# Sparse attention and a gated feed-forward layer: shared value buffers, dense rows in stage order, another load order, and gathers by indirect transfer

## The chip, the core and the metric

The kernel runs on one core of one Trainium2 chip. The core has five engines that run at the same time, each with its own queue of instructions that it takes strictly in order: TensorE (PE, matrix products and transposes), VectorE (DVE), ScalarE (ACT), GpSimd (POOL) and SyncE (SP), which computes nothing and only issues transfers. Semaphores tie the queues together. The metric is the device time of one execution in microseconds; lower is better.

## The reference

Four batches of eight heads, 768 positions of 64 numbers each. The positions fall into 24 blocks of 32. A query block sees its own block and both neighbours, the first and the last block, and three blocks drawn at random; the first and the last query block see everything:

```python
mask = np.abs(blk_i - blk_j) <= 1
mask = mask | (blk_i == 0) | (blk_j == 0) | (blk_i == 23) | (blk_j == 23)
for qb in range(24):
    for kb in sampled_blocks[qb]:
        mask[qb*32:(qb+1)*32, kb*32:(kb+1)*32] = True
scores = np.where(mask, scale * q @ k.T, -1e9)
attn_out = softmax(scores) @ v
x = attn_out, heads side by side: (3072, 512)
out = (sigmoid(x @ w_gate) * (x @ w_val)) @ w_out        # 512 -> 1536 -> 512
```

All inputs are float32; the kernel computes in 16 bits and accumulates in float32.

## The kernel before, in words

**A planner writes the order.** The kernel builds a list of operations (`P(name, engine, duration, function, deps, prio, ...)`) and simulates them (`Planner.run`, lines 69 to 178). Each has an engine or a choice of two, an assumed duration, dependencies that must have ended (`deps`), dependencies that must only have been issued (`after`), a priority, and buffers that it takes and gives back (`acq`, `rel`). The program is then emitted in the order of the simulation. On the chip each engine follows that list, and waits where the data are not there or a buffer is not free. An `after` is a matter of the list alone, and makes no wait on the chip.

**Attention, one batch after another** (`attention`, lines 430 to 785). `load` (line 348) brings K, Q and V of a batch from float32 in DRAM to 16 bits in one of three stage buffers `stg` (96 partitions; partition p holds rows 8p to 8p+7), issued on POOL. PE transposes K and Q (line 456), DVE or ACT copy the results to `KT` and `QT` (lines 466 to 474). V is rearranged by DVE (`vsh`, line 486), in batch 0 into the space of `XL`, later into another stage buffer, and SP writes it to a scratch area `scr` in DRAM, 768 KB in four transfers (`f_scr`, line 495). From there SP loads three things:

- `VN`, all values of the batch, for the dense rows (line 500);
- windows: for three or four query blocks at once the three neighbouring value blocks, into `V1` (line 542). Each batch has two windows at a time, called A and B; even and odd batches have their own pair (`r = b % 2`);
- gathers: for each query block its three random value blocks, into `V2`, by three transfers whose addresses come from registers (line 587).

The first and the last value block go to one window by DMA (lines 514, 515) and are copied by POOL to the other places (line 522).

For each of the 22 sparse query blocks `i` of a batch, POOL copies the three random key blocks to `KG` (line 573; the first and last block stand there already, lines 530, 531). PE adds a mask row by four small matmuls (line 608) and the scores by eight (line 614), DVE takes the maximum (line 626), ACT the exponential (line 635), DVE the reciprocal, DVE or POOL the scaling (lines 643 to 655), PE transposes (line 666), DVE or ACT copy to `PTS` (line 673), PE multiplies with `V1` and `V2` (line 686), ACT or DVE put the result into `XT` (line 701). Mostly two blocks go as one step. Six `P` buffers and two `PTS` buffers bound how many blocks may be under way.

The dense rows (first and last query block, per pair of heads `p`) have scores against all 768 keys (line 714), softmax, six transposes of 128 columns (line 751), a copy to `DPT` (line 756) and six products with `VN` (line 764). In batch 0 they come at its end, in the others at its start.

**Feed-forward**, in eight groups of 128 to 512 rows: products with `wg` and `wv` (line 814), tanh and combination (lines 822, 827), the product with `wo` (line 840), scaling, and the store, which SP issues (line 854). A group can start when its rows of `XT` are there; the planner puts the groups between attention steps, and the last two mostly behind. The weights come on POOL's queue, in four pairs of chunks and three chunks of `wo` (lines 371, 379). `GATES` (line 295) puts some of them behind the gathers of blocks 7, 9, 10 and 11 of batch 0 in the list.

Where the change and the steps touch the code:

Of the kernel before, what the change touches and what calls it, by code (L numbers as in the profile page):

```python
# [18 lines left out]
BLK = 32  # L19
# [5 lines left out]
TP = 96  # L25
# [156 lines left out]
def kernel(  # L182
# [28 lines left out]
    cst = np.zeros((1, NB, 8), np.float32)  # L211
# [3 lines left out]
    cst_h = nc.inline_tensor(cst, name="bb_cst")  # L215

# [14 lines left out]
    ones = sb("ones", [128, 128], bf16)  # L231
    cst_t = sb("cst", [1, NB, 8], f32)
    sbi = sb("sbi", [1, NB * 3 * 2], i32)
    kidx = sb("kidx", [1, 128], i32)
    vidx = sb("vidx", [1, 128], i32)
# [12 lines left out]
    VN = sb("VN", [128, 6, DM])  # L248
    V1 = {(r, x): sb(f"V1{r}{x}", [128, n, DM]) for r in range(2) for x, n in (("A", 4), ("B", 3))}
    V2 = {(r, x): sb(f"V2{r}{x}", [128, n, DM]) for r in range(2) for x, n in (("A", 4), ("B", 3))}  # L250
# [9 lines left out]
    DPT = [sb(f"DPT{s}", [128, S]) for s in range(2)]  # L260
# [17 lines left out]
    XT = [sb(f"XT{g}", [128, NP, 128 * len(G)]) for g, G in enumerate(GROUPS[:-2])]  # L278
    XT += [XL[:, 0:NP, :], XL[:, NP : 2 * NP, :]]
    V0 = XL.rearrange("p a n -> p (a n)")[0:TP, 0 : H * TJ * D]  # L280
# [6 lines left out]
    W0 = [(4, 4, "A"), (8, 3, "B"), (11, 4, "A"), (15, 3, "B"), (18, 2, "A"), (1, 3, "B"), (20, 3, "A")]  # L287
    W1 = [(1, 3, "B"), (20, 3, "A"), (4, 3, "B"), (7, 4, "A"), (11, 3, "B"), (14, 4, "A"), (18, 2, "B")]
# [7 lines left out]
    WCH, WOH = 4, 3  # L296
    SCALE_ENG, SCALE_DUR = ("POOL", "DVE"), (0.9, 0.42)
# [5 lines left out]
    def f_const_dma(o):  # L303
        pin(nc.sync.dma_start(sbi, sampled_blocks.bitcast(i32).rearrange("(x a) b -> x (a b)", x=1)))
        pin(nc.sync.dma_start(cst_t, cst_h.ap()))
        pin(nc.sync.dma_start(ident, ident_h.ap()))

    c_dma = P("cdma", "SP", 1.9, f_const_dma, prio=-100, lat=2.2)
# [5 lines left out]
    def f_mask(o):  # L314
# [17 lines left out]
        pin(V.tensor_scalar(mrow[0:1, :, 2:5], in0=m3, scalar1=NEG, scalar2=None, op0=ALU.mult))  # L332
        pin(V.tensor_scalar(mrow[0:1, :, 0:2], in0=cst_t[:, :, 3:5], scalar1=NEG, scalar2=None, op0=ALU.mult))
# [74 lines left out]
    FF = {"w": None, "vn": None}  # L408
# [21 lines left out]
    def attention(b, prio0, ldeps):  # L430
# [5 lines left out]
        if b == 0:  # L436
            ldk, hk = load("k", k, b, pp - 0.050, ldeps, np_)
            ldq, hq = load("q", q, b, pp - 0.049, ldk[-1:], np_)
            ldv, hv = load("v", v, b, pp - 0.048, ldq[-1:])
            FF["w"] = weights(ldv[-1])  # L440
        else:
            ldv, hv = load("v", v, b, pp - 0.050, ldeps)
            ldk, hk = load("k", k, b, pp - 0.049, ldv)
            ldq, hq = load("q", q, b, pp - 0.048, ldk)
# [39 lines left out]
        def f_vsh(o):  # L484
            t = by_head(stg[pl.handles[hv][1]])
            pin(nc.vector.tensor_copy(by_row(V0 if b == 0 else stg[o.slots[f"vsh{b}"][1]]), t.rearrange("p h j d -> p j h d")))

        vs = P(f"vsh{b}", "DVE", 1.14, f_vsh, deps=ldv, prio=pp - 0.045, rel=[hv],
               acq=[(f"vsh{b}", [("v0", 0)] if b == 0 else stages)])

        def f_scr(o):
            src = V0 if b == 0 else stg[o.slots[f"vsh{b}"][1]]
            dst = scr[b].rearrange("(b j c) n -> c b j n", j=TJ, c=4)
            for c in range(4):
                pin(nc.sync.dma_start(dst[c], src.rearrange("(b c) (j n) -> c b j n", c=4, j=TJ)[c]))

        sc = P(f"scr{b}", "SP", 2.0, f_scr, deps=[vs], prio=pp - 0.045, dma=2.2, ndma=3, rel=[f"vsh{b}"])

        def f_vn(o):
            pin(nc.sync.dma_start(VN, scr[b].rearrange("(t p) n -> p t n", p=128)))  # L500

        vn = P(f"vn{b}", "SP", 0.5, f_vn, deps=[sc], after=[FF["vn"]], prio=bp - 1.2 + (0.5 if b == 0 else 0), dma=2.3,
               acq=[(f"vn{b}", [("vn", 0)])])
        FF["vn"] = vn

        steps = S0 if b == 0 else S1
        wins = W0 if b == 0 else W1
        step_of = {i: y for y, st in enumerate(steps) for i in st}
        wprio = {}
        for i0, n, x in wins:  # L510
            wprio.setdefault(x, bp + 0.1 * step_of[i0] - 1.5)
        vfl = {}
        def f_fl(o):
            pin(nc.sync.dma_start(V1[r, "A"][96:128, 0, :], scr[b][0:BLK, :]))
            pin(nc.sync.dma_start(V2[r, "A"][0:BLK, 0, :], scr[b][S - BLK : S, :]))

        fl = P(f"vfl{b}", "SP", 1.0, f_fl, deps=[sc] + v_users[b - 2], prio=min(wprio.values()) - 0.05, dma=0.2, ndma=2)
        for x, n in (("A", 4), ("B", 3)):
            def f_fc(o, x=x, n=n):
                n0 = 1 if x == "A" else 0  # L520
                for vt, ps in ((V1, slice(96, 128)), (V2, slice(0, BLK))):
                    pin(nc.gpsimd.tensor_copy(
                        vt[r, x][ps, n0:n, :].bitcast(f32),
                        vt[r, "A"][ps, 0:1, :].bitcast(f32).broadcast_to([BLK, n - n0, DM // 2])))

            vfl[x] = P(f"vfc{b}{x}", "POOL", 2.0, f_fc, deps=[fl], prio=wprio[x] - 0.05)

        def f_kfl(o):
            for s in range(NKG):
# [370 lines left out]
```

## Time and profile before

| | us |
|---|---|
| median of the runs (367.83 to 373.71) | 369.97 |
| the profiled execution | 371.52 |
| its span, first to last instruction | 369.6 |
| TensorE busy | 326.2 |
| VectorE busy | 256.0 |
| ScalarE busy | 218.3 |
| GpSimd busy | 106.8 |
| mean granted TensorE clock | 0.957 |

A page of the profile gives busy time by engine, forty slices of the span (each digit the busy tenths of a slice of 9.24 us), the chain of work that ended last, and groups of instructions by source line with what ended the idle time before them. Further views are cut from the same trace: busy time by stage, one engine's instructions in order of time, waits, and transfers. An engine name with a q (SPq, POOLq) stands for instructions that only issue or count and are not busy time.

### The profile page before, as it was taken

What the parts mean: (1) busy time and instruction counts of PE and PEld (TensorE: products, weight loads), DVE (VectorE), ACT (ScalarE), POOL (GpSimd) and SP (SyncE); (2) the same over time, 40 slices, a digit from 0 to 9 for tenths busy, and PEclk for the clock granted to TensorE, in tenths of its full rate; (3) what the DMA queues carried; (4) which work ended last, traced back from release to release, by engine and by line L of the source; (5) the groups of instructions that cost most, each with busy time, mean ns of one, the idle gap of its engine ahead of it and who ended that gap; (6) DMA issues with size and microseconds to landing.
All of it is one profiled execution on the core that took longest, in us unless ns stands there. A gap on an engine that the chain in (4) does not pass through costs nothing.

```text
span 369.6 us, 11338 instructions
## 1 busy us (share of the span) xinstructions
PE 326.2 (88%) x3904; PEld 203.1 (55%) x3904; DVE 256.0 (69%) x686; ACT 218.3 (59%) x662; POOL 106.8 (29%) x361
## 2 busy tenths in 40 slices
PE   2745968989789689999799999999999999999995
PEld 2634756757666544566366556555655654444442
DVE  8697747778688869689469999668989833402320
ACT  3566546774687746767477777877775653313321
POOL 8457470116333553212005234002574100000000
PEclk9995789999999869999899999999999999999999
DMA  7947899997979893125343623331133430011002
GB/s 123 205 115 208 156 212 231 218 243 157 228 188 203 165 268 73 45 67 162 101 118 109 168 73 98 115 94 38 46 89 87 139 104 2 1 59 57 0 30 86
DMA packets 47262, 45.09 MB, mean 122 GB/s; under 512 B 5986, under 2 KB 44132, under 8 KB 47204
## 3 DMA queue, kind: packets, MB, share of 16 engines
q1 hardware_dynamic: 31956, 30.20, 28.8%
q0 software_dynamic: 15248, 14.16, 24.4%
q8 instruction: 31, 0.51, 0.6%
q14 instruction: 27, 0.22, 0.2%
HBM read 49.06 MB, written 9.44 MB: 158 GB/s over the span
## 4 chain that ended last, share of the span: by engine, by line
PE 63%; DVE 14%; DMA 11%; issue 4%; ACT 4%; SPq 2%; POOL 0%; POOLq 0%; DVEq 0%; ACTq 0%
PE bank L814 28%; PE bank L840 17%; PE bank L686 4%; DMA stg<-in_q_dram 4%; PE bank L614 4%; DVE NM L626 4%; PE bank L666 4%; PE bank L608 3%; DVE P L654 2%; DMA wv<-in_moe_w_val_dram 2%; DMA V10A<-scr 2%; DVE HT L827 2%; DMA V21A<-scr 2%; DMA scr<-stg 1%; DVE m L326 1%
## 5 line engine op out<-in xcount | busy, mean ns | idle before, releaser
L635 ACT ACTIVATE P<-bank,NM 128x256 f16<-128x256 f32 x176 | 81.5, 473 | 27.2 <-DVE NM L626 22.1
L827 DVE SCALAR_TENSOR_TENSOR HT<-TH,bank 128x512 f16<-128x512 f32 (+2 forms) x96 | 52.6, 551 | 48.2 <-PE bank L814 43.5
L822 ACT ACTIVATE TH<-bank 128x512 f32<-128x512 f32 (+2 forms) x96 | 46.9, 493 | 54.8 <-PE bank L814 46.0
L573 POOL COPY KG<-KT 128x64 f32 x264 | 51.0, 239 | 96.5 <-PE bank L614 89.1
L840 PE MATMUL bank<-wo,HT 128*128 128x512 f16 x288 | 66.8, 386 | 3.3 <-ACT YS L849 2.5
L626 DVE TENSOR_REDUCE NM<-bank 128x2 f32<-128x512 f32 x88 | 59.0, 684 | 3.7 <-PE bank L614 3.2
L814 PE MATMUL bank<-XT,wv 128*128 128x512 f16 (+2 forms) x288 | 55.2, 316 | 2.1 <-DMA wv<-in_moe_w_val_dram 2.0
L814 PE MATMUL bank<-XT,wg 128*128 128x512 f16 (+2 forms) x288 | 55.5, 317 | 0.8 <-DMA wg<-in_moe_w_gate_dram 0.3
L814 PEld LDWEIGHTS <-wv 128*128 128x128 f16 x384 | 32.9, 99 | 27.3 <-DMA wv<-in_moe_w_val_dram 2.1
L840 PEld LDWEIGHTS <-HT 128*128 128x128 f16 x288 | 27.7, 99 | 35.4 <-issue 5.9
L814 PEld LDWEIGHTS <-wg 128*128 128x128 f16 x384 | 32.5, 100 | 25.8 <-issue 1.9
L654 DVE TENSOR_SCALAR P<-P,ZZ 128x256 f16<-128x256 f16 x150 | 38.3, 300 | 2.3
L608 PE MATMUL bank<-mrow,ones 128*64 128x96 bf16 (+2 forms) x352 | 26.1, 227 | 11.4 <-ACT P L635 8.5
L635 ACT ACTIVATION_READ_ACCUMULATOR P<-bank,NM 128x1 f32 x176 | 35.7, 203 | 0.0
L614 PE MATMUL bank<-KG,QT 128*64 128x160 f16 x352 | 34.3, 249 | 0.1
L614 PE MATMUL bank<-KT,QT 128*64 128x96 f16 x352 | 32.0, 218 | 0.4 <-ACT QT L474 0.4
L666 PE MATMUL bank<-ident,P 128*128 128x128 f16 x352 | 29.3, 229 | 2.3 <-ACT QT L474 1.3
L673 DVE COPY PTS<-bank 128x1024 f16<-128x1024 f16 (+1 forms) x37 | 23.6, 643 | 10.6 <-PE bank L666 10.5
L608 PEld LDWEIGHTS <-ones 128*64 128x64 bf16 x352 | 16.5, 115 | 25.7 <-issue 13.3
L849 ACT ACTIVATE YS<-bank 128x512 f32<-128x512 f32 x20 | 11.9, 597 | 29.4 <-PE bank L840 22.7
L614 PEld LDWEIGHTS <-QT 128*64 128x64 f16 x704 | 27.6, 119 | 0.9 <-ACT QT L474 0.7
L666 PEld LDWEIGHTS <-P 128*128 128x128 f16 x352 | 23.6, 103 | 8.1 <-issue 3.0
(91 smaller groups left out, 476.0 us busy)
## 6 DMA issues: line engine op xcount, KB each, us to landing
out_dram<-YS SPq DMA_DIRECT2D x24, 256.0 KB
stg<-in_v_dram POOLq DMA_DIRECT2D x4, 768.0 KB, 10.3
VN<-scr SPq DMA_DIRECT2D x4, 768.0 KB
V20A<-scr SPq DMA_DIRECT2D x74, 32.0 KB
stg<-in_k_dram POOLq DMA_DIRECT2D x3, 768.0 KB, 10.5
stg<-in_q_dram POOLq DMA_DIRECT2D x3, 768.0 KB, 14.8
scr<-stg SPq DMA_DIRECT2D x12, 192.0 KB
V21A<-scr SPq DMA_DIRECT2D x68, 32.0 KB
```

The costliest lines, as they stand in the source:

```text
L573: pin(nc.gpsimd.tensor_copy(t[:, :, (2 + n) * BLK : (3 + n) * BLK].bitcast(f32), KT[r].bitcast(f32)[:, :, bass.ds(vals[(i % 8) * 3 + n], B ...
L608: pin(nc.tensor.matmul(t[64 * hp : 64 * hp + 64, a, 256 - w : 256], ones[:, 0:64], mv, start=(a == 0), stop=False, skip_group_check=True))
L614: pin(nc.tensor.matmul(t[64 * hp : 64 * hp + 64, a, c0:c1], QT[r][:, p, 1 + i, :], src[:, p, :], start=False, stop=True, skip_group_check= ...
L626: pin(nc.vector.tensor_reduce(NM[o.slots[hz][1]][:, 0:2], t, axis=AX.X, op=ALU.max, negate=True))
L635: pin(nc.scalar.activation(pb[:, a, :], t[:, a, :], AF.Exp, bias=NM[z][:, a : a + 1], scale=1.0, accum_out=ZZ[z][:, a : a + 1]))
L654: pin(nc.vector.tensor_scalar(pb[:, a, :], in0=pb[:, a, :], scalar1=ZZ[z][:, a : a + 1], scalar2=None, op0=ALU.mult))
L666: pin(nc.tensor.transpose(t[:, u * 512 + c * 128 : u * 512 + c * 128 + 128], pb[:, c * 128 : c * 128 + 128], ident))
L673: pin(copy(o)(PTS[pl.handles[hTS][1]][:, 0:n], banks[o.slots[hT][1]].bitcast(f16)[:, 0:n]))
L814: pin(nc.tensor.matmul(t, wt[:, c, f_ * 128 : f_ * 128 + 128], XT[g][:, c, :], start=(c == 0), stop=(c == 3)))
L822: pin(nc.scalar.activation(TH[o.slots[ht][1]][:, 0:n], banks[o.slots[hg][1]][:, 0:n], AF.Tanh, bias=0.0, scale=0.5))
L827: pin(nc.vector.scalar_tensor_tensor(HT[:, f_, hoff : hoff + n], in0=TH[o.slots[ht][1]][:, 0:n], scalar=1.0, in1=banks[o.slots[hv][1]][:, ...
L840: pin(nc.tensor.matmul(t, HT[:, f_, hoff + tt * 128 : hoff + tt * 128 + 128], wo[:, f_, :], start=(f_ == 0), stop=(f_ == NF - 1)))
```

## The change

1. **Four value buffers for all batches.** The A and B windows of even and odd batches become four buffers 0 to 3 that the windows take in turn through all batches (sizes 4, 3, 4, 3 blocks). In `V2` the random blocks now stand in partitions 0 to 95 and the last block in 96 to 127; the columns of `KG` are reordered to match. The first and last block are loaded once per batch into `FL`, and POOL copies them into each buffer before its first use in the batch, which comes after the last product of the batch before in that buffer.
2. **Dense rows on values in stage order.** `VN` and its load go. The rearranged values stay in SBUF in `VR` (two buffers, batches by turn; the first is the space of `XL`), 96 partitions and eight groups, and the dense rows run over eight groups of 96 keys instead of six of 128. The dense scores read the keys in that order, in runs of four elements. The shuffle of V no longer needs a second stage buffer; it waits for `VR` to be free.
3. **Load order in batch 0: K, V, Q** instead of K, Q, V, and the first weight chunk stands behind the write to `scr` in the list.
4. **Batches 2 and 3 gather by indirect transfer:** POOL issues one per query block, with 96 row numbers from a table `rows`, instead of three on SP. The table is worked out on DVE at the start.
5. **The mask** of a block takes two matmuls of 192 columns instead of four of 96. `KG`'s fixed blocks are copied slot by slot.
6. **Room:** the `XT` buffers of groups 0, 1, 2 and 5 share one space; group 5 waits for the first three groups, groups 6 and 7 for batch 2's dense rows and its write to `scr`.

The diff, cut to its core:

```diff
+    place_h = nc.inline_tensor((np.arange(96, dtype=np.float32) % BLK).reshape(96, 1), name="bb_place")
...
-    VN = sb("VN", [128, 6, DM])
-    V1 = {(r, x): sb(f"V1{r}{x}", [128, n, DM]) for r in range(2) for x, n in (("A", 4), ("B", 3))}
+    NVB = 4
+    V1 = [sb(f"V1{x}", [128, 4 - x % 2, DM]) for x in range(NVB)]
+    FL = sb("FL", [128, 2, DM])
...
-    V0 = XL.rearrange("p a n -> p (a n)")[0:TP, 0 : H * TJ * D]
+    VR = [XL.rearrange("p a n -> p (a n)")[0:TP, 0 : H * TJ * D], sb("VR1", [TP, H * TJ * D])]
...
+    VGATHER = [("SP", 1.5)] * 2 + [("POOL", 1.1)] * 2
...
+            pin(V.tensor_scalar(rows[x, :], in0=sbb[x, 2 * n : 2 * n + 6 * (NB - 1) + 1 : 6], scalar1=BLK, scalar2=place[x, 0:1],
+                                op0=ALU.mult, op1=ALU.add))
...
-            ldq, hq = load("q", q, b, pp - 0.049, ldk[-1:], np_)
-            ldv, hv = load("v", v, b, pp - 0.048, ldq[-1:])
-            FF["w"] = weights(ldv[-1])
+            ldv, hv = load("v", v, b, pp - 0.049, ldk[-1:])
+            ldq, hq = load("q", q, b, pp - 0.048, ldv[-1:], np_)
+            FF["w"] = weights(ldq[-1])
...
-        vs = P(f"vsh{b}", "DVE", 1.14, f_vsh, deps=ldv, prio=pp - 0.045, rel=[hv],
-               acq=[(f"vsh{b}", [("v0", 0)] if b == 0 else stages)])
+        vs = P(f"vsh{b}", "DVE", 1.14, f_vsh, deps=ldv + scr_ops[-2:-1] + dpvs.get(b - 2, []), prio=pp - 0.045, rel=[hv], acq=[(f"vr{b}", [("vr", r)])])
...
-            pin(nc.sync.dma_start(VN, scr[b].rearrange("(t p) n -> p t n", p=128)))
...
+        if b == 0:
+            FF["gate"][0].after.append(sc)
...
+        turn = [(FF["nw"] + y) % NVB for y in range(len(wins))]
+            o = P(h, "SP", 0.5, f_w, deps=[sc], prio=wp, after=[prevw.get(x)], acq=[(h, [("V", x)])], dma=0.28 * n)
+            if x not in filled:
+                def f_fc(o, x=x, n=most[x]):
+                    for c, vt in ((0, V1), (1, V2)):
+                        pin(nc.gpsimd.tensor_copy(
+                            vt[x][96:128, 0:n, :].bitcast(f32),
+                            FL[96:128, c : c + 1, :].bitcast(f32).broadcast_to([BLK, n, DM // 2])))
+
+                filled[x] = P(f"vfc{b}{x}", "POOL", 1.8, f_fc, deps=[fl] + win_pv[x][-1:], prio=wp - 0.05)
...
                 def f_vg(o, i=i, x=x, ws=ws):
+                    if o.eng == "POOL":
+                        pin(nc.gpsimd.indirect_dma_start(
+                            V2[x][0:96, ws, :], None, scr[b][:, :], bass.IndirectOffsetOnAxis(ap=rows[:, i : i + 1], axis=0)))
+                        return
...
-                vg = P(f"vg{b}_{i}", "SP", 1.5, f_vg, ...)
+                vg = P(f"vg{b}_{i}", *VGATHER[b], f_vg, ...)
...
-                    for a in range(2):
-                        for hp in range(2):
-                            pin(nc.tensor.matmul(t[64 * hp : 64 * hp + 64, a, 256 - w : 256], ones[:, 0:64], mv,
-                                                 start=(a == 0), stop=False, skip_group_check=True))
+                    for hp in range(2):
+                        pin(nc.tensor.matmul(t[64 * hp : 64 * hp + 64, :, 96 + n0 * BLK : 96 + n1 * BLK], ones, mv,
+                                             start=True, stop=False, skip_group_check=True))
...
-                                         KT[r][:, p, c0 : c0 + 384], start=True, stop=True))
+                                         KT[r][:, p, :].rearrange("d (b j c) -> d j b c", j=TJ, c=4)[:, c0 // TP : c0 // TP + 4],
+                                         start=True, stop=True))
...
-                for c in range(6):
-                    pin(nc.tensor.transpose(t[:, c * 128 : c * 128 + 128], d[:, c * 128 : c * 128 + 128], ident))
+                for j in range(TJ):
+                    pin(nc.tensor.transpose(t[0:TP, j * 128 : j * 128 + 128], d[:, j * TP : j * TP + TP], ident))
...
-                for c in range(6):
-                    pin(nc.tensor.matmul(t, VN[:, c, p * 128 : p * 128 + 128], d[:, c * 128 : c * 128 + 128], start=(c == 0), stop=(c == 5)))
+                for j in range(TJ):
+                    pin(nc.tensor.matmul(t, VR[r][:, j * DM + p * 128 : j * DM + p * 128 + 128], d[:, j * 128 : j * 128 + 128],
+                                         start=(j == 0), stop=(j == TJ - 1)))
```

## The prediction

> **What bounds the kernel now.** I read the page first: busy shares and the slices.
>
> ```profile
> PE 326.2 (88%) x3904; PEld 203.1 (55%) x3904; DVE 256.0 (69%) x686; ACT 218.3 (59%) x662; POOL 106.8 (29%) x361
> ...
> PE   2745968989789689999799999999999999999995
> ...
> PEclk9995789999999869999899999999999999999999
> DMA  7947899997979893125343623331133430011002
> ```
>
> PE is the bound from about 140 us on (slice 15); what it idles lies mainly before, and so do two of the three regions of slow clock. So I asked for the busy time by stage (columns: PE, weight loads, DVE, ACT, POOL, then clock, DMA share, GB/s).
>
> ```profile
> 20.00:32.00 12.00, 4.82 (x81) 3.67 (x76) 11.72 (x35) 8.07 (x34) 7.40 (x26) 0.80 0.47 138
> 32.00:41.00 9.00, 7.62 (x106) 6.58 (x106) 6.07 (x19) 5.22 (x22) 3.73 (x14) 0.51 1.04 226
> 44.00:52.00 8.00, 3.81 (x67) 3.05 (x65) 3.79 (x11) 3.38 (x13) 8.00 (x19) 0.94 1.07 165
> 94.00:101.00 7.00, 4.59 (x62) 3.72 (x59) 3.99 (x15) 4.46 (x13) 3.28 (x4) 1.00 1.22 228
> 123.00:137.00 14.00, 10.61 (x111) 6.57 (x110) 10.32 (x26) 7.31 (x24) 8.95 (x26) 0.63 1.09 216
> 165.00:300.00 135.00, 130.56 (x1610) 78.37 (x1605) 111.21 (x314) 94.97 (x295) 38.50 (x143) 0.99 0.37 102
> ```
>
> From 20 to 32 VectorE is full (11.72 of 12) while the DMA is half idle; then PE works at half clock; at 44 to 52 and in the two stages after it PE waits with the DMA busy. From 165 to 300 PE is full and POOL has 96 us free. The chain says for what PE waits: weights, then gathered values; the Q load on it is batch 2's.
>
> ```profile
> 44.43 6.85 DMA wv<-in_moe_w_val_dram
> ...
> 91.23 14.79 DMA stg<-in_q_dram
> ...
> 124.21 5.96 DMA V21A<-scr
> ```
>
> SP's own queue shows why the values are late: they reach scr only at 18.6, and with two windows per batch the third window's load (38.54) waits for the first product, with nine gathers queued behind it.
>
> ```profile
> 18.59 3.51 SPq L495 DMA_DIRECT2D scr<-XL  x4
> ...
> 30.56 0.47 SPq L500 DMA_DIRECT2D VN<-scr  x1
> 31.22 2.90 SPq L587 DMA_DIRECT2D V20A<-scr  x6
> 38.54 0.34 SPq L542 DMA_DIRECT2D V10A<-scr  x1
> 39.07 5.88 SPq L587 DMA_DIRECT2D V20B<-scr  x9
> ```
>
> **The parts and the sum.** Profiled execution: span 369.6, in all 371.5, which is 1.55 over the median 369.97. Terms in us; ends in brackets.
>
> *a. Q after V, batch 0: +3.5 [0, +6.5].* K's two halves start their transposes at 6.40 and 8.46, Q's first at 10.44: about 2.0 per half load, so V ahead of Q costs 4.1. Some is slack already: the second Q half's transposes waited at 12.05 for VectorE, not for the load. In the new order VectorE has ended the mask (11.5, with three more operations of about 0.2) before Q lands, so those operations cost nothing; were Q early, they would cost 0.6. That leaves +2.5 to 3; I add up to a microsecond because scr's writes now run beside Q's second half. Batch 2's Q took 14.79 beside SP traffic, against 4.1 for K alone, hence the high end, with scr's writes ahead of it by their own 4.
>
> The Trainium skill, "DMA: Bandwidth & Descriptors", section "Queues, rings and completion order", speaks against the new order: a DMA engine takes turns between the queues that have work. By that rule all of scr's 768 KB could go ahead of Q's end, at K's pace 4.1 us, and this term would be +6.5 and the sum 3 worse; the 14.79 fits it.
>
> *b. The value shuffle leaves the full stretch: -1.2 [-1.2, 0].* It ran 1.21 at 17.36, between the first two maxima, on the path; now it runs near 12.5, while VectorE waits for Q.
>
> *c. Batch 0's values and the weights: -7 [-13, 0].* Scr starts near 13.8 instead of 18.6, and the window that held up nine gathers finds one of four buffers free, so the wait at 34 to 38.5 goes. Weight chunks are listed on POOL behind gathers 7, 9, 10 and 11 in the plan and move up with them, into the stretch where the DMA share is 0.47. What can go: PE's 4.2 idle at 44 to 52, 1.5 at 62 to 64 (behind a gather's issue), about 2 of the gaps at 32 to 36, and half of the slow-clock work of 32 to 41 and 51 to 54 (some 5). I take half, as the DMA is full from 48 to 80 and the bytes are nearly the same. The first weight pair, moved behind scr, lands about where it did: it stood behind K, Q and V anyway.
>
> *d. No VN load, more buffers, in batch 1: -6 [-9, 0].* Each VN load is 768 KB, at K's pace 4 us of a full DMA; three of the four fall in full stretches, the last at 202 is hidden. Between 94 and 101 PE idles 2.4 for gathers; between 123 and 137 it idles 3.4 and runs 8 at half clock, 3 to 4 lost. Two thirds go. V's shuffle also needs no stage slot any more, so batch 1's values reach scr before 82.9, and batch 2's Q no longer waits for scr (91.2). The new wait, shuffle 2 behind batch 0's last dense product (118), holds only a stage slot; batch 2 is not used before 180.
>
> *e. SP free of gathers in batches 2 and 3: -2 [-4, 0].* The gap at 178 to 180.5 (2.5 idle, then slow clock, 1.7) ends with an output store that SP issued late, behind gathers of batch 1 and before batch 2's; half may stay.
>
> *f. PE's own work: +3.2 [+1, +9].* Dense rows take eight transposes and eight products per head pair instead of six and six. Twelve transposes take 0.81 (114.44 to the next matmul at 115.25), twelve products 0.76: four more per pair cost 0.26, by 16 pairs +4.2. The mask is two matmuls of 192 columns instead of four of 96; the four start within 0.07 and the keys 0.11 after the first, and the columns are the same, so 0.01 to 0.03 of each of 88 goes: -1 [-3, 0]. The dense scores read keys in runs of four elements. No row shows that. Nearest are the contiguous reads (two matmuls of 384 columns in 0.33) and the mask's broadcast row (four of 96 in 0.11), neither of them slow; I take 0, and at most double, 32 x 0.16 = +5.
>
> *g. POOL, ACT, DVE: 0 [0, +7].* Sixteen more fills of 0.83 are 13 us of POOL; 44 gathers replace 132 issues on SP (0.32 each). An indirect transfer is not in the trace: POOL's own DMA issues take 0.67 to 0.95, its longest instruction 2.80. I take 1.1, the plan's figure, because the plan's other POOL figures match their rows (0.56 against 0.59 for three copies, 0.8 against 0.78 for a load). 48 us fit into the 96 free. A gather that waits for its window holds the key copies behind it on POOL, and those hold the scores; PE then has feed-forward work. If POOL gives up its ten scalings at 250 to 290 (1.04 each), VectorE takes them at 0.6: 35.6 plus 6 of 40, over full, hence the +7. DPT copies of 1024 instead of 768 columns add 0.13 on VectorE or 0.2 on ACT sixteen times, hidden by PE. Copying KG's fixed blocks per slot moves 32 copies and changes no count.
>
> Sum: 3.5 - 1.2 - 7 - 6 - 2 + 3.2 + 0 = -9.5. That is 362.0 from the profiled execution, 360.5 from the median; I forecast **361**.
>
> **Rivals.** *Gains stay in the queues, 0.27:* the DMA is full at 48 to 80 whatever the order, Q's delay is paid at once, and the plan's list keeps PE behind the same weights. For it: shares over 1.0 in four of the six stages; against: 0.47 before. Then c is -2, d -3, e -1: 371.5 + 3.5 - 1.2 - 6 + 3.2 = 371.0, by the median 369.5, same.
>
> *POOL becomes the bound in batches 2 and 3, 0.19, slower:* 135 us hold 38.5 of POOL and 7 new fills, so it decides from (135 - 45.5) / 44 = 2.0 per gather. At 2.8, its longest row, 44 x 0.8 = 35 more, less the 9.5: about 397 by the profiled execution; at 2.4 it is +18 and 380. For it: one VectorE operation on 72 elements took 4.55 (its neighbours 0.22) while POOL issued loads and cleared QT, so the two do block each other. Against: POOL's DMA issues never pass 0.95, VectorE full or not.
>
> The Trainium skill, "SBUF — State Buffer", section "Who interferes with whom", has the rule for it: some VectorE copies and scalings shut GpSimd out of a shared port, descriptor writing included. By it the gathers stretch where VectorE is 97% busy (200 to 230); the issue rows so far do not.
>
> *The change doesn't do what it says, 0.06:* strided reads cost the +5, or values come early but the list places products no earlier (c gone): 366 to 369, same.
>
> **Numbers.** Forecast 0.48 (352 to 362.5), no gain 0.33 with the last rival (362.5 to 377), slower 0.19 (377 to 397). Two per cent, 7.4 us, is about what a measurement can tell from no change, so these are also faster 0.48, same 0.33, slower 0.19. For 8 in 10 the range goes from 351 to 380, which takes in POOL at 2.4 per gather; the forecast's own is 352 to 366.
>
> **What would show it.** First scores at 19 to 20 instead of 15.3; the first product near 28 instead of 33.0; the wait for wv at 44 under 3; no half clock near 126 to 136; dense groups of eight; indirect issues on POOL near 1.1 with KG's waits still on PE. Wrong if POOL is over 80% busy after 165, if PE's idle before 140 (33.8 now) is still over 30, or if the dense scores exceed 0.33 per pair.

## The result, and the profile after

The changed kernel took **386.22 us** (median of 4 runs, 384.71 to 389.72), the kernel before 369.98 (four runs, three of which were known when the prediction was made): ratio **1.047** (95% interval 1.038 to 1.057), slower. The forecast was 361 with a range of 351 to 380, so it was wrong. Measured again four times, on three chips, the same program took 365.7 to 366.4, ratios 0.986 to 0.990; on which chip the first measurement ran is not recorded. So two things have to be explained: the 20 us between the first measurement and the repeats, and, in the repeats, why the gain was some 4 us and not the 9.5 of the sum.

The page of the first measurement (execution 384.71, span 382.6):

```profile
PE 327.8 (86%) x3792; PEld 205.4 (54%) x3792; DVE 265.9 (69%) x688; ACT 217.0 (57%) x677; POOL 156.8 (41%) x414
...
PE   1476869999888999999499987978999999999995
...
PEclk9995998999999899999799999999999999999999
DMA  7987999999949743232521131340232010011002
```

PE's work hardly grew (326.2 to 327.8). Before, its slices were full from the sixteenth on but for a 7 at the twentieth; now the twentieth (182 to 191 us) is a 4, and from 220 on come 8, 7, 9, 7, 8. POOL is at 41% of the span, and at 74.34 of 135 us in the last long stage of the table below, so it is not the bound. The same stages as in the prediction, and 176 to 192 (columns: PE, weight loads, DVE, ACT, POOL, then clock, DMA share, GB/s):

```profile
20.00:32.00 12.00, 8.27 (x117) 7.08 (x117) 10.60 (x27) 6.17 (x25) 9.40 (x28) 0.89 0.86 184
32.00:41.00 9.00, 6.98 (x95) 5.74 (x94) 6.69 (x21) 8.08 (x28) 6.43 (x20) 0.58 0.94 173
44.00:52.00 8.00, 6.02 (x118) 5.09 (x116) 7.26 (x25) 6.38 (x26) 7.58 (x24) 1.00 1.25 192
94.00:101.00 7.00, 6.33 (x108) 5.04 (x107) 6.17 (x17) 6.10 (x19) 1.75 (x3) 1.00 1.13 204
123.00:137.00 14.00, 11.94 (x130) 6.78 (x131) 10.04 (x29) 8.40 (x31) 2.91 (x15) 0.88 0.79 201
165.00:300.00 135.00, 117.34 (x1297) 69.62 (x1296) 103.78 (x275) 78.83 (x262) 74.34 (x165) 0.97 0.27 77
176.00:192.00 16.00, 9.67 (x85) 5.73 (x84) 7.36 (x22) 6.36 (x24) 9.98 (x17) 0.82 0.45 120
```

Most stages up to 137 improved in the way that was forecast (44 to 52: 3.81 to 6.02 of 8; 94 to 101: 4.59 to 6.33 of 7; clock at 123 to 137 from 0.63 to 0.88); from 32 to 41 PE still runs at a clock of 0.58 (0.51 before). The loss is in the last long stage: 117.34 of 135 instead of 130.56. The chain names two places there:

```profile
45.06 11.45 DMA wv<-in_moe_w_val_dram
...
117.90 6.27 DMA V<-scr
...
183.80 5.53 issue
...
253.03 5.50 another core or an unknown queue
```

The wait for `wv` and that for gathered values are still there (PE itself waits 2.2 us for `wv`, 2.0 before). The two pieces at 183.80 and 253.03 are new, and are put down to nothing that the profile shows. At the first of them, PE's instructions and then VectorE's:

```profile
180.18 0.79 PE L747 MATMUL bank<-KT,QT 128*128 128x384 f16 x2
...
181.05 2.75 PE L882 MATMUL bank<-wo,HT 128*128 128x512 f16 x12
189.33 1.04 PE L747 MATMUL bank<-KT,QT 128*128 128x384 f16 x2 [5.53 <-issue]
```

```profile
180.92 0.15 DVE L672 RECIPROCAL ZZ<-ZZ 128x2 f32<-128x2 f32 x1
183.91 0.56 DVE L758 TENSOR_REDUCE NM<-bank 128x1 f32<-128x384 f32 x1 [2.84 <-PE bank L882]
185.26 0.56 DVE L758 TENSOR_REDUCE NM<-bank 128x1 f32<-128x384 f32 x1 [0.79 <-PE bank L882]
```

PE has issued both dense score products (line 747) by 180.97, but VectorE starts on the first at 183.91 and on the second at 185.26: PE's signals come 3 and more microseconds late. (The profile names line 882 as the releaser since the signals arrive just as its products end, at 183.80; the scores are in other banks, and in the repeat below the same signals arrive while line 882 runs.) ScalarE and SP wait in the same way, until PE itself lacks what they owe it. Meanwhile POOL issues its indirect transfers (line 613) without a break, nine from 178.2 to 189.0, one each 1.23 us; the second stretch, at 256, lies at the end of a row of seven (248.6 to 256.9). The same stretch in a repeat of the same program (execution 367.49), PE and VectorE:

```profile
182.39 0.49 PE L747 MATMUL bank<-KT,QT 128*128 128x384 f16 x2
182.72 0.38 PE L695 MATMUL bank<-ident,P 128*128 128x128 f16 x4
182.94 2.75 PE L882 MATMUL bank<-wo,HT 128*128 128x512 f16 x12
185.53 0.49 PE L747 MATMUL bank<-KT,QT 128*128 128x384 f16 x2
```

```profile
182.80 1.00 DVE L758 TENSOR_REDUCE NM<-bank 128x1 f32<-128x384 f32 x2
```

VectorE begins 0.41 after the product has started and PE goes on without a gap, though the same nine transfers pass at the same pace (180.4 to 191.2). Set side by side instruction by instruction, since the order is the same, the first measurement is 1.9 us ahead at 181, 5.8 behind after the first row, 10.7 behind at 235, 15.5 behind after the second row and 17.0 at the end.

### The profile page after: what moved, and what is told of

It reads as the page before. It is cut to its first block, busy times and chain, and to the rows that moved or that the text cites. A ratio compares the mean times of both kernels' runs of the same rounds, so it can differ in the third digit from the quotient of the medians.

```text
span 382.6 us, 10768 instructions
## 1 busy us (share of the span) xinstructions
PE 327.8 (86%) x3792; PEld 205.4 (54%) x3792; DVE 265.9 (69%) x688; ACT 217.0 (57%) x677; POOL 156.8 (41%) x414
## 4 chain that ended last, share of the span: by engine, by line
PE 57%; DVE 15%; DMA 11%; issue 6%; SPq 5%; ACT 2%; another core or an unknown queue 1%; POOL 1%; POOLq 0%; ACTq 0%; DVEq 0%
PE bank L851 28%; PE bank L882 10%; PE bank L715 4%; DMA V<-scr 4%; PE bank L695 4%; PE bank L643 3%; DMA wv<-in_moe_w_val_dram 3%; PE bank L637 3%; DMA stg<-in_v_dram 3%; DVE P L683 2%; SPq L618 2%; DMA scr<-XL 2%; DVE NM L655 2%; DVE HT L864 2%
## 5 line engine op out<-in xcount | busy, mean ns | idle before, releaser
L882 PE MATMUL bank<-wo,HT 128*128 128x512 f16 x288 | 65.8, 382 | 0.8 <-DVE HT L864 0.8
L851 PE MATMUL bank<-XA,wv 128*128 128x512 f16 (+2 forms) x288 | 54.3, 312 | 3.0 <-DMA wv<-in_moe_w_val_dram 2.2
L851 PE MATMUL bank<-XA,wg 128*128 128x512 f16 (+2 forms) x288 | 55.2, 316 | 1.1 <-DVE XA L730 0.8
L683 DVE TENSOR_SCALAR P<-P,ZZ 128x256 f16<-128x256 f16 x164 | 47.6, 337 | 2.4
L613 POOL DMA_INDIRECT V<-scr,rows x44 | 41.3, 938 | 18.6 <-issue 14.8
L715 PE MATMUL bank<-PTS,V 128*128 128x64 f16 x704 | 31.1, 197 | 8.6 <-DMA V<-scr 4.1
L715 PEld LDWEIGHTS <-V 128*128 128x128 f16 x704 | 27.6, 101 | 18.2 <-issue 7.4
L555 POOL COPY V<-FL 32x1024 f32<-32x1024 f32 (+1 forms) x32 | 28.9, 939 | 12.6 <-DMA V<-scr,rows 3.9
L637 PE MATMUL bank<-mrow,ones 128*64 128x192 bf16 (+1 forms) x176 | 26.0, 284 | 8.0 <-ACT P L664 6.4
L643 PEld LDWEIGHTS <-QT 128*64 128x64 f16 x704 | 31.2, 120 | 0.7 <-ACT QT L501 0.7
```

The lines of the kernel that those rows point to most:

```text
L613: pin(nc.gpsimd.indirect_dma_start(V2[x][0:96, ws, :], None, scr[b][:, :], bass.IndirectOffsetOnAxis(ap=rows[:, i : i + 1], axis=0)))
L643: pin(nc.tensor.matmul(t[64 * hp : 64 * hp + 64, a, c0:c1], QT[r][:, p, 1 + i, :], src[:, p, :], start=False, stop=True, skip_group_check= ...
L683: pin(nc.vector.tensor_scalar(pb[:, a, :], in0=pb[:, a, :], scalar1=ZZ[z][:, a : a + 1], scalar2=None, op0=ALU.mult))
L715: pin(nc.tensor.matmul(t[:, u, p, :], vt[:, ws, p * 128 : p * 128 + 128], pt[:, off : off + 64], start=(c == 0), stop=(c == 1), skip_group ...
L851: pin(nc.tensor.matmul(t, wt[:, c, f_ * 128 : f_ * 128 + 128], XT[g][:, c, :], start=(c == 0), stop=(c == 3)))
L882: pin(nc.tensor.matmul(t, HT[:, f_, hoff + tt * 128 : hoff + tt * 128 + 128], wo[:, f_, :], start=(f_ == 0), stop=(f_ == NF - 1)))
```

## The experiments

Two theories stood against each other at first: **A**, the indirect transfers on POOL are the loss, and **B**, the shared value buffers with their fills on POOL are. Ratios are to the kernel before, run on the same chip.

**1. All gathers on SP again (e1_sp).**

```diff
-    VGATHER = [("SP", 1.5)] * 2 + [("POOL", 1.1)] * 2
+    VGATHER = [("SP", 1.5)] * 4
```

> The changed kernel with the values of all four batches gathered by SP from registers, three 32-row transfers for each query block as before; everything else of the change stays. Theory A (the indirect transfers on POOL are the loss: while POOL issues 9 and 7 of them in a row, at 178 to 189 and 249 to 257 us, PE stands still for 5.5 and 3.8 us): the two idle stretches go, PE's idle after 140 us falls from 23.6 back to about 10 to 14, and the time to 367 to 373. Theory B (the loss is in the four shared value buffers, their fills on POOL that hold up DVE's scalings, and DVE's extra work): the time stays at 380 to 388, with other gaps in the place of those two.

368.08 us, 0.999 (0.995 to 1.002). The two stretches are gone, as A expected, and everything else of the change together is not to be told from nothing.

**2. The same order, ordinary transfers in place of indirect ones (e2_plain).**

```diff
-                        pin(nc.gpsimd.indirect_dma_start(
-                            V2[x][0:96, ws, :], None, scr[b][:, :], bass.IndirectOffsetOnAxis(ap=rows[:, i : i + 1], axis=0)))
+                        pin(nc.gpsimd.dma_start(
+                            V2[x][0:96, ws, :], scr[b][0:96, :]))
```

> The changed kernel with its order of instructions unaltered on every engine; only each of the 44 indirect transfers on POOL (96 rows from the places in a list) is an ordinary transfer of 96 rows x 1 KB, issued by POOL at the same place, from the first 96 rows of the value scratch. What it leaves out: the values of the sampled blocks in batches 2 and 3 are those of the first blocks. Theory A1 (it is the indirect form that stalls the other engines): the gaps of 5.5 and 3.8 us go and the time is 368 to 375. Theory A2 (it is that POOL's queue carries the gathers and delays what stands behind them: key copies, fills, stage loads): the gaps stay in some form and the time is 380 to 388.

365.26 us, 0.990 (0.988 to 0.993), no stretch, and below the 368 that A1 began at. POOL's groups for line 613, of this kernel and of the first measurement:

```profile
L613 POOL DMA_DIRECT2D V<-scr x44 | 22.6, 518 | 8.9 <-issue 6.4 <-DVE NM L655 1.8
```

```profile
L613 POOL DMA_INDIRECT V<-scr,rows x44 | 41.3, 938 | 18.6 <-issue 14.8
```

An indirect issue holds POOL 0.94 us, an ordinary one 0.52. At this point the indirect form itself looked like the culprit.

**3. Indirect transfers in batch 3 alone (e3_b3).**

```diff
-    VGATHER = [("SP", 1.5)] * 2 + [("POOL", 1.1)] * 2
+    VGATHER = [("SP", 1.5)] * 3 + [("POOL", 1.1)]
```

> The changed kernel with indirect transfers in batch 3 alone, and batch 2 gathered by SP. Theory A: the stall near 184 us goes and one near 250 us stays, so the time falls by some 5 to 8 of the 16 us, to 377 to 381. Theory B: no change, 382 to 388.

368.84 us, 1.000 (0.995 to 1.005), below what either theory expected: the half of the loss that was to stay is not there. This kernel has nine indirect transfers in a row, from 236 to 247, and PE works through them (11.05 of 12 us). A row alone does not do it.

**4. A part of the 44 indirect, and then the others (f1_bursts, f2_rest).** Order unaltered; the first keeps the two rows indirect, the second, with `not` before the condition, the other 28.

```diff
+                        NTH[0] += 1
+                        pin(nc.gpsimd.indirect_dma_start(V2[x][0:96, ws, :], None, scr[b][:, :], bass.IndirectOffsetOnAxis(ap=rows[:, i : i + 1], axis=0)) if 4 <= NTH[0] <= 12 or 26 <= NTH[0] <= 32 else nc.gpsimd.dma_start(V2[x][0:96, ws, :], scr[b][0:96, :]))
```

> The changed kernel, every engine's order unaltered; only the 16 indirect transfers of the two long rows (the nine issued from 178 to 188 us and the seven from 249 to 256) stay indirect, the other 28 are ordinary 96-row transfers from the first rows of the value scratch (so the sampled blocks' values there are those of the first blocks). Instruction for instruction, the changed kernel loses 8 us at the first row and 4 at the second against the kernel in which all 44 are ordinary, and 6 elsewhere. Theory rows (the loss sits where many indirect transfers follow each other): 365.3 + 12 = 375 to 380. Theory each (every indirect transfer costs its share, 20 / 44 = 0.45 us): 365.3 + 7 = 371 to 374.

> The complement: those 16 are ordinary transfers, the other 28 stay indirect; order unaltered; the values of the 16 blocks' samples are left out in the same way. Theory rows: 365.3 + 6 = 369 to 373, and no gap near 184 or 256. Theory each: 365.3 + 13 = 376 to 380.

364.15 us, 0.981 (0.975 to 0.988), and 365.11, 0.984 (0.978 to 0.991). Both theories of these two expectations, "rows" and "each", fell: neither the rows nor the others cost anything.

**5. All 44 indirect, with a later release (f3_lag1, g2_lag2).** A gather of batches 2 and 3 also waits for the scores of one step, or two steps, before (`hist` collects them by step). The planner makes a new order for either kernel.

```diff
-                vg = P(..., deps=[sc, regop[b, "SP", part]], ...)
+                vg = P(..., deps=[sc, regop[b, "SP", part]] + (hist[-1] if b > 1 and si >= 1 else []), ...)    # lag2: hist[-2], si >= 2
```

> The changed kernel with all 44 indirect, but each gather of batches 2 and 3 also waits for the scores of the step before its own, so that the row of seven in batch 3 falls into pieces of one to three; in batch 2 a row of seven stays. PE's and POOL's order is planned anew. Theory rows: at least the 4 us near 256 go, 376 to 382. Theory each: 383 to 389. If the later gathers are late for their products: over 389.

> All 44 indirect, each gather of batches 2 and 3 also behind the scores of two steps before; the row of nine in batch 2 stays whole, the row of seven in batch 3 falls apart. Theory number with this order (long rows decide once all 44 are indirect): 376 to 382, with the stretch near 184 idle. Theory place: 366 to 371, as with the shorter wait (367.7).

367.71 us, 0.991 (0.987 to 0.995), and 366.20, 0.986 (0.978 to 0.994). The first is faster than every theory had it. The second is where "place" had it, the theory that the first measurement's chip or hour is the cause; to test that, the changed kernel itself was measured again.

**6. The changed kernel again (g1_again, h1_again, h2_again, i2_again).** No edit.

> The changed kernel itself, unaltered, once more. Neither half of the indirect transfers alone costs anything (the kernels with 16 and with 28 of the 44 were both near 365 us), and 44 of them with one wait more were at 367.7. Theory number (all 44 together, in this order, are the loss): 384 to 390 again. Theory place (the 386 us belong to the chip or the hour at which it was measured and not to the kernel): 366 to 371, with no idle stretch of PE near 184 and 256.

> The changed kernel a third time. It took 386.2 us when it was first measured (4 runs, 384.7 to 389.7) and 366.2 in the second measurement on another chip (365.4 to 368.1). Theory place: 365 to 369 again, or 384 to 390 again where this chip does what the first one did; nothing between. Theory chance (its time scatters from run to run over the whole stretch): values between 369 and 384.

> The changed kernel once more, beside the three that follow and on their chip. Theory place: 364 to 369 as on two chips of three, or 384 to 390 with PE idle near 184 and 256 as on the first.

> The changed kernel a fifth time, beside it: 364 to 368, or 384 to 390 if the first measurement's state is met again.

366.22, 365.74, 366.36 and 365.73 us; ratios 0.986 (0.979 to 0.993), 0.990 (0.986 to 0.995), 0.990 (0.986 to 0.994) and 0.988 (0.982 to 0.994). The idle stretches are in none of the four profiles. The 386 us belong to the first measurement, in all four of its runs, and not to the program as such; whether to its chip, its hour or something else is not shown. Theory A is thereby not refuted for that measurement, since the stretches lie at the rows of indirect transfers; but what had to come together there could not be found, as it did not come back.

**7. Each gather as two indirect transfers of half rows (i1_split).** Row numbers count half rows, and `rows2` holds those of the second halves. This doubles what a gather holds of POOL.

```diff
-                        pin(nc.gpsimd.indirect_dma_start(
-                            V2[x][0:96, ws, :], None, scr[b][:, :], bass.IndirectOffsetOnAxis(ap=rows[:, i : i + 1], axis=0)))
+                        for y, at in enumerate((rows, rows2)):
+                            pin(nc.gpsimd.indirect_dma_start(
+                                V2[x][0:96, ws, y * 256 : y * 256 + 256], None, scr[b].rearrange("s (h n) -> (s h) n", h=2),
+                                bass.IndirectOffsetOnAxis(ap=at[:, i : i + 1], axis=0)))
```

> The changed kernel with each of the 44 gathers as two indirect transfers of 96 half rows (512 B), so that POOL is held twice: 0.92 + 0.30 us once more per gather, some 2.45 us instead of 1.23 and 54 us more in all. The forecast's rival (POOL becomes the bound in batches 2 and 3, from 2.0 us per gather) gives 380 at 2.4 us. If POOL's queue still lies beside PE: 366 to 369. If many indirect transfers are what delayed the other engines' semaphores in the first measurement: idle stretches of PE near the rows, and 380 to 400.

395.14 us, 1.067 (1.057 to 1.077). Here the forecast's slower rival is seen at work, in PE's waits from 160 to 330 us (in all, times, longest), in the page's group, and in PE's instructions:

```profile
PE bank L647 <- POOL KG L592: 18.6, 5, 13.1
```

```profile
L616 POOL DMA_INDIRECT V<-scr,rows x88 | 81.7, 928 | 26.4 <-issue 24.1
```

```profile
258.72 0.21 PE L647 MATMUL bank<-KT,QT 128*64 128x96 f16 x2
272.06 0.34 PE L647 MATMUL bank<-KG,QT 128*64 128x160 f16 x2 [13.13 <-POOL KG L592]
```

A half-row transfer holds POOL as long as a whole-row one (0.93, and 0.30 before it), so a gather costs 2.46; fourteen such transfers, seven gathers, stand in a row from 254.6 to 271.4, and the key copy behind them is 13.1 us late. The expectation had 380 for this case, and by the rival's own sum 2.46 per gather gives some 382; measured are 395. Against the repeat of 367.49 the span is 25.7 us longer: PE idles 20.5 more, 18.6 of it for `KG`, and is busy 5.2 more, with the granted clock at 0.66 from 260 to 280. The rival spread POOL's load evenly over the stage; in a queue that works in order, the row was late in one piece. In the first measurement of the changed kernel no wait of PE for `KG` is among those from 160 to 330: its loss was another one.

**8. The first loads as K, Q, V again, with gathers on SP (e4_sp_kqv) and in the changed kernel (k2_kqv).**

```diff
-            ldv, hv = load("v", v, b, pp - 0.049, ldk[-1:])
-            ldq, hq = load("q", q, b, pp - 0.048, ldv[-1:], np_)
-            FF["w"] = weights(ldq[-1])
+            ldq, hq = load("q", q, b, pp - 0.049, ldk[-1:], np_)
+            ldv, hv = load("v", v, b, pp - 0.048, ldq[-1:])
+            FF["w"] = weights(ldv[-1])
```

> As the kernel with all gathers on SP, and the first loads again in the order K, Q, V. If Q behind V only costs (the forecast's term a, +3.5) and what V gains is lost in the queues: first scores at 15.3 instead of 19.4 and 2 to 4 us faster than that kernel. If V's earlier arrival is worth the forecast's term c (up to 7): 1 to 4 us slower. If both hold: within 1 us.

> The changed kernel with the first loads in the order K, Q, V again. The forecast's terms a (+3.5, Q behind V) and c (-7, V, value scratch and weights earlier) say 3.5 us slower than the changed kernel: 368 to 371. Where SP gathered, the old order was 1 us faster: then 364 to 366.

With gathers on SP 366.95 us, 0.995 (0.991 to 0.998), not to be told from the 0.999 of experiment 1. In the changed kernel 369.36, 1.000 (0.997 to 1.003), against 0.990 (0.986 to 0.994) on the same chip: 1% or some 3.5 us slower, as much as terms a and c of the forecast give together. In part that agreement is luck: before 140 us PE idles 33.0 in it, inside the repeats' 32.8 to 35.0, at a granted clock of 0.90 instead of 0.93 or 0.94, and from 165 to 200 it idles 2.7 instead of 0.8, where neither term put anything. The planner makes a new order behind the loads in both kernels, so what the load order is worth depends on that order.

**9. Without the fills of the value buffers in batches 1 to 3 (f4_nofill with gathers on SP, j1_nofill in the changed kernel).**

```diff
-                    for c, vt in ((0, V1), (1, V2)):
+                    for c, vt in ((0, V1), (1, V2)) if b == 0 else ():
```

> The kernel with all gathers on SP, without the fills of the value buffers in batches 1 to 3 (24 of POOL's 32 wide copies; the first and last block's values in those batches are then batch 0's). If POOL's fills hold up DVE's scalings and the products: 2 to 5 us faster than with them (368.1), and DVE's scalings back from about 0.33 to 0.30 us on the mean. If they lie beside other work: within 1 us.

> The changed kernel without the 24 fills of the value buffers in batches 1 to 3 (their first and last block's values are then batch 0's); every other instruction stays in its order. The forecast set POOL's, ACT's and DVE's term g at 0 with an upper end of +7, and the kernel came out some 6 us above the sum of its terms on the chips where it took 366. If the fills are that term, as where SP gathered (1.8% there): 359 to 362, some 0.97 to 0.98 of the kernel before. If not: 365 to 367.

363.74 us, 0.980 (0.975 to 0.986), against 0.999 for experiment 1: 1.8% or 7 us. In the changed kernel 362.94, 0.980 (0.976 to 0.985), against 0.986 to 0.990: some 2 to 4 us. That is less than the 6 that the expectation looked for, and probably more than nothing: its interval lies clear of two of the four repeats' and overlaps the other two. The mechanism stands in the repeat's instructions, POOL's and VectorE's, and in VectorE's without the fills:

```profile
153.06 2.03 POOL L555 COPY V<-FL 32x1024 f32<-32x1024 f32 x2 [0.96 <-PE bank L851]
```

```profile
153.14 2.03 DVE L683 TENSOR_SCALAR P<-P,ZZ 128x256 f16<-128x256 f16 x2
```

```profile
153.24 0.48 DVE L683 TENSOR_SCALAR P<-P,ZZ 128x256 f16<-128x256 f16 x2
```

Two fills and two scalings take the same 2.03 us; without the fills the scalings take 0.48. PE had idled 0.48 us when its next transposes of `P` started at 155.23, 0.06 behind the second scaling. In the whole execution VectorE's scalings are busy for 46.2 us with the fills and 43.3 without; no matmul of PE waits for a fill itself, and one weight load does, for 2.0 us. The Trainium skill, "SBUF — State Buffer", section "Who interferes with whom", says that such VectorE scalings can take the pair of ports that GpSimd uses, and that whichever issues first has it for its whole instruction while the other is shut out. The trace agrees for the fills. It does not for the issue of indirect transfers, where the prediction had named the rule: in the same repeat they took 0.92 to 1.12, median 0.93, however busy VectorE was.

**10. The fills by SP from the value scratch (k1_fill), and with K, Q, V (k3_both).**

```diff
+                        if o.eng == "SP":
+                            src = scr[b][c * (S - BLK) : c * (S - BLK) + BLK, :]
+                            src = bass.AP(tensor=src.tensor, offset=src.offset, ap=[[DM, BLK], [0, n], [1, DM]])
+                            pin(nc.sync.dma_start(vt[x][96:128, 0:n, :], src))
+                            continue
```

> The changed kernel, the fills of the value buffers in batches 1 to 3 made by SP's transfers straight from the value scratch (two for each buffer, the 32 rows read n times), not by POOL's copies; batch 0 keeps POOL's. If the 24 wide copies on POOL cost what leaving them out gained where SP gathered (some 6 us, 368.1 to 363.7 on two chips): 360 to 363. If that gain came from the products that no longer wait for a fill, which SP's transfers make wait as well: 364 to 367. If SP's queue, with each fill behind the products of the batch before, now holds up windows and stores: over 367.

> Both edits at once, K, Q, V and the fills by SP. If both gain as expected: 358 to 362, and faster than both kernels by more than 1%. If they share one gain: 361 to 364.

368.11 us, 0.995 (0.991 to 0.999), and 369.34, 0.998 (0.995 to 1.002); the changed kernel on that chip 0.990. VectorE's and POOL's load fell, the time did not; both edits together missed both ranges of their expectation. From 140 to 165 the first of them does free PE, which idles 0.4 us instead of 1.2, with VectorE at 20.7 of 25; but before 140 its granted clock is 0.90 instead of 0.93 or 0.94. So what leaving the fills out gains is not had by moving them to SP, where each waits for the products of the batch before; that this wait is the reason is likely and not shown. Neither beats the changed kernel as the repeats have it.

## Why the prediction was wrong

**In the first measurement the step that failed is term g**, what POOL, ScalarE and VectorE cost PE in batches 2 and 3: put at 0 and at most +7. PE idles 17.7 us from 165 to 300 instead of 4.4, 13.2 more. Nothing in the sum held signals that come late, and the mechanism that the prediction had for a loss there is not the one that came. The slower rival needed 2.0 us per gather; a gather took 0.94 + 0.30, near the 1.1 taken, and the rival duly stayed away: no wait for key copies. The 17 us between the first measurement and a repeat of the same program come from signals that arrived late while POOL issued indirect transfers, in two stretches (7.6 us from 181 to 195, the slow clock behind the gap included, 4.0 at 256) and in pieces between. That this did not recur in thirteen further measurements with indirect transfers of whole rows (experiments 3 to 6 and 8 to 10) is shown. What set it off is open: the chip, its neighbours or the hour were not varied on purpose, and every execution here has its span recorded, so the recording itself cannot be left out as a cause either.

The traces hold one thing more, the semaphores' own records, which no view above prints. In the repeat, PE's records stand 0.02 us behind the instructions that signal; in the first measurement there is none from 179.89 to 183.82, while five such instructions end from 180.32 to 181.19. And records are lost: of the 1104 for the landing of POOL's transfers, the first measurement has 735, the four repeats 1084 to 1088, and the kernel of experiment 2, with ordinary transfers in the same places, all. Every other kernel with whole-row indirect transfers lacks some (3 to 30), and none without them lacks any; in experiment 4 the 16 transfers of the two rows go with 18 lost records, the other 28 with 3. So a weak form of a disturbance goes with the indirect transfers, in rows above all, in every measurement; whether lost records and late signals have one cause is not shown.

**In the repeats, 366, the forecast was 5 us too low.** Busy time by stretch, the kernel before and then the repeat of 367.49, one execution each (columns as above):

```profile
0.00:44.00 44.00, 25.61 (x427) 21.43 (x428) 35.94 (x89) 23.22 (x73) 26.23 (x87) 0.84 0.84 167
44.00:101.00 57.00, 46.74 (x718) 36.81 (x716) 38.98 (x119) 34.72 (x119) 20.05 (x48) 0.97 1.11 208
101.00:140.00 39.00, 33.88 (x496) 22.42 (x495) 32.72 (x93) 27.35 (x86) 17.32 (x60) 0.87 0.95 207
140.00:165.00 25.00, 24.95 (x337) 14.39 (x337) 19.95 (x50) 17.12 (x55) 4.70 (x24) 1.00 0.20 50
165.00:200.00 35.00, 31.82 (x379) 19.23 (x374) 25.84 (x76) 21.96 (x58) 7.25 (x25) 0.95 0.42 120
```

```profile
0.00:44.00 44.00, 20.94 (x335) 17.75 (x336) 30.99 (x73) 20.41 (x59) 28.76 (x81) 0.84 0.88 161
44.00:101.00 57.00, 49.69 (x829) 39.52 (x827) 46.39 (x144) 40.04 (x138) 18.83 (x54) 1.00 1.16 218
101.00:140.00 39.00, 34.34 (x470) 22.77 (x467) 31.42 (x84) 27.61 (x90) 19.16 (x59) 0.91 0.80 172
140.00:165.00 25.00, 23.80 (x356) 15.22 (x353) 24.43 (x59) 17.47 (x57) 12.97 (x44) 1.00 0.29 77
165.00:200.00 35.00, 34.19 (x413) 21.24 (x412) 29.67 (x82) 25.16 (x78) 19.56 (x41) 1.00 0.39 115
```

PE's idle time changed by +4.7, -3.0, -0.5, +1.2 and -2.4 us, and by -0.5 from 200 to 300. The clock column adds an estimate of what no longer ran slowly: 0.03 of 57, 0.04 of 39 and 0.05 of 35, some 5 us together. The span fell by 4.0.

- **a, Q after V (+3.5): right in kind, some 1 us short.** First scores at 19.4 (first measurement) and 19.7 (repeat) instead of 15.3; PE idles 4.7 us more in the first 44 (3.1 to 5.0 in the four repeats), which also holds what later values cost there. The +6.5, with the write to `scr` ahead of Q, did not come: in this repeat POOL's queue moves 0.41 MB, the size of Q's second half, from 14 to 16 us, and the write's first bytes come after 16.
- **b, the value shuffle (-1.2): not to be seen apart.** VectorE has 30.99 instead of 35.94 in the first stretch, but PE was waiting for Q there.
- **c and d, earlier values and weights, no VN load (-13): the step that failed in the repeats.** They are the stretches from 44 to 140: 3.5 us of idle time and an estimated 3.3 of slow clock, some 7. How they share it is not shown. The values' way shows where c went wrong. SP's queue before, in the first measurement and in the repeat:

```profile
18.59 3.51 SPq L495 DMA_DIRECT2D scr<-XL  x4
25.74 0.35 SPq L514 DMA_DIRECT2D V10A<-scr  x1
```

```profile
14.44 3.51 SPq L520 DMA_DIRECT2D scr<-XL  x4
24.21 0.34 SPq L532 DMA_DIRECT2D FL<-scr  x1
```

```profile
14.80 4.37 SPq L520 DMA_DIRECT2D scr<-XL  x4
26.68 0.34 SPq L532 DMA_DIRECT2D FL<-scr  x1
```

  The write to `scr` starts 4.2 us earlier in the first measurement (14.44 for 18.59), but the first load behind it only 1.5 (24.21 for 25.74): 9.8 us from write to read instead of 7.2. In the repeat it is 11.9, and the first load comes at 26.68, later than before, as in three of the four repeats (26.7 to 26.9; 23.8 in the fourth). The packets in the trace show what was beside the write: between its issue and that first load POOL's queue moved 0.15 MB before, 1.02 in the first measurement and 0.93 to 1.13 in the repeats, most of it, 0.73 to 0.75 in these two traces, from 20 to 26 us. That is about the size of the first weight pair (768 KB), which POOL issues at 16.64, when the write has been issued and has not landed; before, the pair was issued at 5.18. The prediction had it land "about where it did". Putting it behind the write in the planner's list orders the issues and makes no wait on the chip. Q is not needed for it: in experiment 8's changed kernel, with Q loaded ahead of V, the write still takes 9.8 (19.64 to 29.45) beside 0.60 MB. A kernel that holds the pair back until the write has landed was not run.

  So the first product came at 30.1 (31.1 to 31.8 in the repeats) and not near 28. The rival "gains stay in the queues" was right in this: PE's idle time before 140 went from 33.8 only to 31.2, and to 32.8 to 35.0 in the repeats, over the 30 that the prediction named as the mark of its own error.
- **e, SP free of gathers (-2): a gain is there, but not for this reason.** From 165 to 200, where the gap behind SP's late store was, PE idles 2.4 us less, and some 1.7 of slow clock goes. But in experiment 1, with SP gathering again, the stretch is just as full:

```profile
165.00:200.00 35.00, 34.17 (x392) 20.82 (x388) 28.64 (x76) 24.73 (x88) 7.76 (x29) 1.00 0.38 105
```

  So something else of the change closed that gap; what did is not shown. Where the gathers stand shows from 200 to 300: PE idles 2.6 us there in experiment 1 and 0.8 to 0.9 in the repeats. In all, gathers on POOL instead of SP are worth 0.9 to 1.3% by the ratios of experiments 1 and 6, taken on different chips.
- **f, PE's own work (+3.2): about half.** The sum of the other measured pieces is -5.5, the span fell by 4.0, so 1.5 remain as an estimate. Strided reads cost nothing: two dense score products still follow each other in 0.33 (182.39 to 182.72).
- **g, POOL, ACT, DVE (0, up to +7): missed.** I had asked whether the fills fit on POOL, which they do, and not what they do to VectorE while they run. From 140 to 165 VectorE is at 24.43 of 25 and PE loses 1.2 (0.1 without the fills); leaving the fills out is worth some 2 to 4 us in all (experiment 9), of which the rest is not traced to single waits.

## What to carry to other kernels

A copy moved to an engine with room is not free if it shuts out another engine that is full: price it by the neighbour's instructions during the copy. A transfer that is started earlier is worth what its reader gains, not what its start gains: look from the write's issue to the first read behind it, and at what else is issued in between. Before a gain is put down to one edit of several, look at the same stretch in a kernel without that edit. And when a slow result shows idle time that the profile gives no cause for, measure the same program again on another chip before explaining it by the change.

## What was not expected of the hardware

- Signals from PE came late by 3 us and more while POOL issued indirect transfers in a row, in one measurement (4 runs) out of five of the same program; in the others the same transfers at the same pace (1.23 us each) cost no such stretch. Records of the landing of POOL's transfers are lost in every trace with whole-row indirect transfers (3 to 30 of 752 to 1104, and 369 in the first measurement), and in none without.
- An indirect transfer costs POOL the same 0.93 + 0.30 us for 96 rows of 1 KB and 96 of 512 B: it is paid by the transfer, not by the byte, between these two sizes.
- One wide fill of 32 partitions stretched a VectorE scaling from 0.28 us (the same scaling without the fills) to 1.05. In the repeat of 367.49, nine of the fifteen scalings beside a fill took 0.5 to 1.1.
